# Exchanging the partition halves of the transposed q: copies on VectorE in the place of DMA transfers

## The chip, the core and the metric

The kernel runs on one core of a Trainium2 chip. The metric is the device time of one execution in microseconds. Before the change it is 370.4 us, the median of three runs (370.34 to 371.06).

A core has five engines, each with an in-order queue of its own: TensorE (PE, matmuls; PEld is its weight load), VectorE (DVE), ScalarE (ACT), GpSimd (POOL) and SyncE (SP). DMA transfers run beside them; here SP issues transposes, swaps and stores, and POOL issues the loads. SBUF and PSUM are memories of 128 partitions; matmul results go to PSUM and are moved on by VectorE or ScalarE.

## What is computed

An attention without softmax (squared ReLU), and then a feed-forward layer with exact GELU:

```
# q, k, v: 8 batches x 12 heads x 448 positions x 64, float32
scores = q @ k.T / sqrt(64)
attn   = maximum(scores, 0) ** 2 / 448
x      = attn @ v                      # then to (8 * 448) x 768
out    = gelu(x @ w_in) @ w_out        # w_in 768 x 2048, w_out 2048 x 768
```

## The kernel before

**Tiling.** The work goes by batch b (8), by group g of four heads (3 to a batch) and by step i (7 to a group). A step computes scores with 64x64 matmuls, of which four use the 128x128 array at once: pairs of heads lie in partitions 0 to 63 and 64 to 127 (`fn_qk`, L741, into the PSUM tile `ps`). ScalarE (L753) or VectorE (L755) makes the ReLU into `a_sq`, VectorE squares it (L762), and after seven steps 28 matmuls multiply by v (L802, into `pav`). Casts of `pav` (L517 on VectorE, L519 on ScalarE) give `xT`. The feed-forward layer follows in pieces that are woven between the attention steps: `psh` (L854) and its GELU (L864), then groups of 256 rows with sums on VectorE (`s_sb`, L1153), products (`pso`, L1172) and passes into `osb` (L1206), which SP stores (L1133). The later batches' first layer (`pb`, L998) and row groups use a scheme with seven products in the place of eight. `osb` has 3 buffers, `ps` and `pav` share 3 PSUM buffers, `psh` and `pso` share 2.

**The transposed q.** Scores need q and k with the head dimension on the partitions. For batches 0 and 1 TensorE transposes them (`tp`, L639 and L611). For batches 2 to 7 DMA does (`add_T_dma`): for each group SP issues a transpose of k into `kT` and one of q into a segment of `qT` (both L666). A segment is 128 partitions by 896 bf16 columns. The segment that the transpose fills (the even one, number 2g) has two of the heads' halves in partitions 0 to 63 and the others in 64 to 127. Both matmul halves need both, so a second segment (2g + 1) holds the same data with the partition halves exchanged. It is made by two transfers of 64x896 within `qT` (L686 and L687), here called the swap of a group: there are 6 x 3 = 18. `q_pair` reads both segments in one access, so a group's first scores wait for its swap (`Tq[b, g, c] = (even, both)`).

**The gates.** Before POOL loads q and k of a later batch over the natural tiles `nq` and `nk`, it makes a small copy (`add_gate`, L709) that waits for the transposes of the batch before. For batch 2 the copy reads the odd segment, which the swap writes; for the later batches it reads the even segment. In batches 3 to 6 POOL's first gate is the one for the last group, so a batch's burst of loads starts when that group's even transpose has landed. SP's next transposes wait for those loads.

**The order.** A small scheduler with planned times for each operation builds the program, but here the order is written out: `ORDER` is a list of words such as `D215` or `S230`, a letter for the engine (P, A, D, G, S for TensorE, ScalarE, VectorE, GpSimd, SP) and the operation's number. `place` follows it, and each engine's queue gets its operations in that sequence. The planned times of an operation (engine, time on the engine, time to the result) therefore change nothing in the built order. `mode="X"` marks SP's transposes and swaps for the planner's account of DMA.

The lines that are named later: L517 and L519 are the two branches of the helper `copy` on VectorE and ScalarE; L463 and L552 are the loads of q and k, L570 those of v, L486 those of w_out; L666 the transposes; L686 and L687 the swap; L709 the gates; L1133 the stores.

Of the kernel before, what the change touches and what calls it, by code (L numbers as in the profile page):

```python
# [69 lines left out]
T_STEP = 1.4  # L70
T_TIME = 3.6
T_LOAD = 1.0
SWAP_STEP = 0.9
SWAP_TIME = 3.0


def cols(half):
# [21 lines left out]
D212 A250 P257 D193 A214 A256 D194 P265 D218 S230 A258 D185 P201 D215 A266 G237 S231 G239 P225  # L99
A202 S233 A203 P276 P279 P267 D226 S235 A277 A227 P291 D280 P288 P294 S236 A268 P356 G240 A295  # L100
D289 G153 G238 P350 A357 G149 P348 G270 A292 A351 P285 P300 P303 G272 A349 P354 G241 A301 P364
A304 A355 P312 P318 P362 A365 P370 D319 D281 A363 D296 P358 A313 D290 A286 P282 P306 A371 P315
# [3 lines left out]
A340 A299 D393 A334 D394 P330 P324 P309 D329 P387 D419 A331 D335 A385 S400 S402 A310 D395 D311  # L106
S386 A325 P342 P336 S401 P321 D397 D388 A343 D332 P421 A322 D337 A323 S403 P423 D420 D338 D422
S405 P446 P443 D341 P449 P425 D424 D344 A450 S404 P427 G413 D444 G275 A426 G409 S406 S389 D447
P429 D326 D428 P452 P455 P345 A456 D453 P440 P437 D445 P431 D430 A441 D560 P433 D346 A347 D432
S435 P473 A438 P461 P470 D434 S436 P509 G407 G408 G410 A471 D474 P513 D448 G412 A462 S542 D457  # L110
A510 G411 P479 D454 P476 P464 G415 A514 P519 D472 D442 G414 A465 D439 P517 A520 D477 P515 A480
D451 A518 S541 P485 P467 P458 A468 P491 A516 S545 P511 D459 A486 D561 P523 A492 D487 S543 A512
D460 P503 P494 P500 D563 A524 P525 D463 S544 A495 D466 P521 D469 A526 D481 P531 S546 D504 A522
D478 P527 A532 D501 P537 D475 S548 A528 D505 P529 D502 A538 D493 S547 P488 P497 P482 S549 A498
D489 P606 G556 P600 G552 G416 P535 A483 A530 G550 P533 D601 G551 A607 D484 A536 G553 D490 G555
P539 D496 G554 D499 P609 G559 P603 P506 G558 A604 D610 G557 P624 A534 P639 D562 P564 A540 D605
A507 P566 A640 D625 D565 D508 P615 P612 P618 D567 P568 A616 D613 P570 D617 A569 D611 D614 P572
S705 D619 P657 D571 P627 P636 S704 P574 D580 D573 A637 D620 P576 D608 A658 D575 S578 A628 P584
D581 S708 D638 D577 P586 D583 S579 D582 P630 D602 P633 P621 S706 D626 A634 D631 P651 A585 S707
P642 P588 D632 D587 A643 S709 D659 P590 D629 A652 A622 D641 D591 P648 A623 D644 P666 P663 A589  # L120
S711 D653 P592 D635 A664 S710 G719 P594 G715 A649 D667 D593 S712 P654 P660 P645 A655 D661 P769
P763 D595 P596 S598 D725 A770 G713 G714 A646 P672 D764 G716 D597 S599 P674 G718 D665 D650 A673
G717 G721 A647 D656 P772 P778 P775 G720 D662 A675 P678 S868 A776 D779 P676 D668 A773 D771 P766
D777 P787 P669 S867 A767 D788 A679 P781 P790 A677 D774 P682 A670 D723 D768 P684 A782 A671 D724
A683 D765 P680 D783 A791 D780 P796 P799 P784 A681 S871 A800 D797 P793 P802 P688 S869 D803 D804
S870 D798 D789 S872 D792 S874 S873 S875 G882 G722 A785 A685 P686 A794 A689 A786 P811 P823 P805
A687 P690 D795 A806 P692 A691 D824 P698 D726 A812 D807 A693 P696 D801 A699 P814 P817 P808 A697
A815 D818 P820 P906 G878 P694 A809 G876 G877 P702 D907 G879 A695 A810 G881 P700 G880 A821 G884
A703 P826 P829 D822 P912 A701 P727 A827 P729 D828 A728 D813 P731 A913 D730 A830 D816 P733 D819
# [3 lines left out]
D923 D926 D754 P757 D932 D908 S980 P939 P948 P927 D758 S981 A940 D949 P960 P945 D941 P835 A928  # L133
S983 D756 D950 A946 P759 A929 S761 D961 S985 D947 P957 P954 P951 A836 D760 S984 A958 D955 P963
P966 P839 D956 A952 S762 D953 S986 A967 P837 D959 A840 P969 D964 P972 P987 A838 D888 P841 A973
P843 D988 D965 A842 D989 P845 A970 D962 A844 D974 P847 D971 A846 D1067 P1002 D968 P990 P975 A1003
# [262 lines left out]
def kernel(  # L399
# [9 lines left out]
    nc = tc.nc  # L409
# [93 lines left out]
    def q_seg(b, n):  # L503

        return get_T(b)[0][:, SEG * n : SEG * n + SEG]
# [9 lines left out]
    def copy(eng, dst, src):  # L515
        if eng == "DVE":
            V.tensor_copy(dst, src)  # L517
        else:
            A.copy(dst, src)  # L519

    def e_copy(n, psum=4):
# [4 lines left out]
    sch = Scheduler({"w": 3, "a": NA, "f": 2, "osb": 3, "s1": 1, "s2": 1, "s3": 1, "s4": 1,  # L526
                     "p": 1})
# [10 lines left out]
    QK, SQ, AV, X, GL = {}, {}, {}, {}, {}  # L538
# [61 lines left out]
    def old_T(b):  # L600
        return [o for (bb, *_), o in QK.items() if bb == b - 2]
# [56 lines left out]
    def add_T_dma(b, after):  # L658


        after = [list(x) for x in after]

        def turn(dst, src, deps):
            return sch.add(
                (("SP", T_STEP, T_TIME),),
                lambda e: nc.sync.dma_start_transpose(dst(), src()),  # L666
                deps + old_T(b) + after.pop(0), mode="X",
            )
# [12 lines left out]

        def swapped(g):
            def fn(e):
                src = q_seg(b, 2 * g)
                to = q_seg(b, 2 * g + 1)
                nc.sync.dma_start(to[:64], src[64:])  # L686
                nc.sync.dma_start(to[64:], src[:64])  # L687

            return fn

        for g in range(G):
            op = turn(k_dst(g), k_src(g), list(ld_k[b, g]))
            for i in range(NK):
                Tk[b, g, i] = (op, op)
            lands = list(dict.fromkeys(ld_q[b, g, c] for c in range(NC)))
            even = turn(q_dst(g), q_src(g), lands)
            both = sch.add(
                (("SP", SWAP_STEP, SWAP_TIME),), swapped(g), [even] + after.pop(0), mode="X"
            )
            for c in range(NC):  # L700
                Tq[b, g, c] = (even, both)

# [839 lines left out]
```

## Time and profile before

| what | value |
|---|---|
| median of 3 runs | 370.4 us |
| the profiled execution: time, span | 370.97 us, 368.8 us |
| ScalarE, GpSimd busy | 52%, 17% |
| granted TensorE clock | full in all slices |
| `qT<-qT` transfers (the swaps) | 36 of 112 KB, 2.5 us median to landing |
| all DMA traffic | 47.10 MB, 128 GB/s mean |
| POOL's waits at the gates for `qT<-nq`, `qT<-qT` | 86.7 us, 21.7 us |
| longest VectorE wait between 120 us and 160 us | 3.17 us, for a store of `osb` |

The page of a profile gives each engine's busy time, the same in 40 slices (a digit is tenths of the slice, 9 is 90% or more), the chain of work that ended last, and groups of instructions by line. A group's row ends with its busy time, the mean ns of one instruction, and the idle time before them with what ended it. In a timeline the columns are start, length (both us), engine, line, operation, what it writes and reads, shapes, count, and in brackets the idle time before it with what ended that. VectorE's lengths overlap: the next instruction can start a little before the recorded end of the one before. DMA-issuing instructions are marked with a q behind the engine's name (SPq); their length is that of the issue, not of the transfer.

### The profile page before, as it was taken

To read this page: it belongs to the slowest core of one execution; us is meant where nothing else is said; L and a number is where in the kernel's file an instruction comes from. 1 tells how busy PE (TensorE), PEld (TensorE's weight loads), DVE (VectorE), ACT (ScalarE), POOL (GpSimd) and SP (SyncE) were. 2 spreads that over 40 slices of the span, in tenths; PEclk is the share of its full clock that TensorE was granted. 3 is DMA by queue.
4 is the path that set the end of the run, shared out by engine and by line. 5 is a ranking of instruction groups with operands and counts; after the bars stand their busy time and mean duration, and the time that the engine had idled before them with its cause. 6 is when DMAs were issued, how large, how long until landed. Compare 5 with 4: busy or idle time off the path is not lost.

```text
span 368.8 us, 8478 instructions
## 1 busy us (share of the span) xinstructions
PE 358.4 (97%) x3560; PEld 222.6 (60%) x3560; DVE 287.8 (78%) x480; ACT 191.9 (52%) x312; POOL 62.3 (17%) x101
## 2 busy tenths in 40 slices
PE   8889999999999999899999999999999999999995
PEld 7665554455544555454555544467898777867663
DVE  3998862589996899698759999999977866667753
ACT  4987868637377544658666366860514124232200
POOL 8565116130240150050051000000000000000000
PEclk9999999999999999999999999999999999999999
DMA  9999999999999999999999970000300202022233
GB/s 166 198 199 201 191 159 145 208 196 187 198 192 195 173 158 171 232 153 192 156 151 222 199 161 2 2 2 0 88 2 0 88 20 67 2 85 87 85 85 88
DMA packets 75046, 47.10 MB, mean 128 GB/s; under 512 B 38528, under 2 KB 71552, under 8 KB 75008
## 3 DMA queue, kind: packets, MB, share of 16 engines
q0 software_dynamic: 32912, 22.47, 42.7%
q1 hardware_dynamic: 41456, 23.59, 32.3%
q8 instruction: 28, 0.46, 0.5%
q10 hardware_dynamic: 640, 0.51, 0.4%
q14 instruction: 10, 0.08, 0.1%
HBM read 45.61 MB, written 11.01 MB: 154 GB/s over the span
## 4 chain that ended last, share of the span: by engine, by line
PE 88%; DMA 5%; DVE 3%; POOL 1%; issue 1%; DVEq 0%; POOLq 0%; SPq 0%
PE pso L1172 29%; PE psh L854 26%; PE pb L998 13%; PE ps L741 9%; PE pav L802 9%; PE pso L1267 3%; DMA out_dram<-osb 3%; DMA v_sb<-in_v_dram 2%; DVE a_sq L762 1%; DVE a_sq L755 1%; DVE osb L1206 1%; POOL nk L552 1%; POOL nq L463 1%; PE tp L639 0%; DVE s_sb L1153 0%
## 5 line engine op out<-in xcount | busy, mean ns | idle before, releaser
L753 ACT ACTIVATE a_sq<-ps 128x896 bf16<-128x896 f32 (+1 forms) x116 | 102.5, 923 | 46.6 <-PE ps L741 43.5
L762 DVE TENSOR_TENSOR a_sq<-a_sq 128x896 bf16<-128x896 bf16 x169 | 97.0, 616 | 7.9 <-ACT a_sq L753 7.7
L854 PE MATMUL psh<-xT,win_sb 128*128 128x448 bf16 (+1 forms) x516 | 96.3, 340 | 0.0
L854 PEld LDWEIGHTS <-win_sb 128*128 128x128 bf16 x516 | 47.9, 98 | 46.1 <-issue 10.0
L755 DVE TENSOR_SCALAR a_sq<-ps 128x896 bf16<-128x896 f32 (+1 forms) x53 | 57.1, 1079 | 18.0 <-PE ps L741 17.8
L1172 PEld LDWEIGHTS <-s_sb 128*128 128x128 bf16 x424 | 40.7, 98 | 25.6 <-issue 1.7
L864 ACT ACTIVATE h_sb<-psh 128x448 bf16<-128x448 f32 x80 | 43.5, 550 | 22.1 <-PE psh L854 21.7
L741 PE MATMUL ps<-qT,kT 64*64 64x448 bf16 (+1 forms) x756 | 47.6, 336 | 1.3 <-issue 0.6
L1035 DVE TENSOR_TENSOR part<-pb,part 128x448 f32<-128x448 f32 x60 | 35.2, 619 | 13.5 <-PE pb L998 11.4
L1172 PEld LDWEIGHTS <-h_sb 128*128 128x128 bf16 x312 | 29.7, 98 | 22.2 <-issue 4.6
L802 PE MATMUL pav<-a_sq,v_sb 64*64 64x448 bf16 (+1 forms) x756 | 36.3, 329 | 2.1 <-issue 1.2
L1172 PE MATMUL pso<-wout_sb,h_sb 128*128 128x384 bf16 x208 | 38.1, 326 | 0.0
L1172 PE MATMUL pso<-wout_sb,s_sb 128*128 128x384 bf16 (+2 forms) x216 | 38.1, 320 | 0.0
L1172 PE MATMUL pso<-t_sb,s_sb 128*128 128x384 bf16 x208 | 38.1, 326 | 0.0
L1206 DVE TENSOR_TENSOR osb<-pso,p_sb 128x384 f32<-128x384 f32 x39 | 21.6, 553 | 15.6 <-PE pso L1172 10.6
L741 PEld LDWEIGHTS <-kT 64*64 64x64 bf16 x756 | 18.5, 105 | 21.1 <-issue 16.2
L802 PEld LDWEIGHTS <-v_sb 64*64 64x64 bf16 x756 | 21.2, 107 | 13.8 <-issue 3.0
L998 PEld LDWEIGHTS <-win_sb 128*128 128x128 bf16 x288 | 27.5, 98 | 2.9 <-issue 0.7
L1044 ACT ACTIVATE h_sb<-part 128x448 bf16<-128x448 f32 x36 | 18.4, 576 | 19.0 <-DVE part L1035 18.9
L519 ACT CAST xT<-pav 128x448 bf16<-128x448 f32 (+1 forms) x38 | 18.3, 500 | 7.8 <-PE pav L802 6.4
L709 POOL COPY gate<-qT 128x16 bf16<-128x16 bf16 x15 | 3.7, 247 | 108.4 <-DMA qT<-nq 86.7
L998 PEld LDWEIGHTS <-ws 128*128 128x128 bf16 x216 | 20.8, 98 | 1.2
(57 smaller groups left out, 298.1 us busy)
## 6 DMA issues: line engine op xcount, KB each, us to landing
nk<-in_k_dram POOLq DMA_DIRECT2D x23, 224.0 KB, 9.2
nq<-in_q_dram POOLq DMA_DIRECT2D x21, 224.0 KB, 9.9
qT<-qT SPq DMA_DIRECT2D x36, 112.0 KB, 2.5
v_sb<-in_v_dram POOLq DMA_DIRECT2D x5, 672.0 KB, 9.8
out_dram<-osb SPq DMA_DIRECT2D x8, 336.0 KB, 3.1
v_sb<-in_v_dram POOLq DMA_DIRECT2D x9, 224.0 KB, 9.7
out_dram<-osb SPq DMA_DIRECT2D x7, 288.0 KB, 3.1
out_dram<-osb SPq DMA_DIRECT2D x8, 240.0 KB, 2.9
```

The costliest lines, as they stand in the source:

```text
L741: nc.tensor.matmul(ps[64 * j : 64 * j + 64, e, x * w : x * w + w], kT[r, g, i * 128 + 64 * j : i * 128 + 64 * j + 64], moving, start=True, ...
L753: A.activation(ar, ps, AF.Relu, scale=c_att)
L755: V.tensor_scalar(ar, ps, c_att, 0.0, op0=mybir.AluOpType.mult, op1=mybir.AluOpType.max,)
L762: V.tensor_mul(box["a2"][:, :, :used], ar, ar)
L802: nc.tensor.matmul(pav[0][o2 : o2 + 64, e, :w], vt[b][r, 2 * g + e, bass.ts(i, D)], box["a2"][r, y, o : o + w], start=(i == 0), stop=(i == ...
L854: nc.tensor.matmul(ph[:, x * n : x * n + n], win_sb[:, kd, bass.ts(m + x, 128)], xT[b][:, kd, c], start=(kd == 0), stop=(kd == KD - 1),)
L864: A.activation(h_ring()[:, m : m + nm, o + c.start : o + c.stop], box[0][:, :S].rearrange("p (x n) -> p x n", x=nm), AF.Gelu,)
L998: nc.tensor.matmul(bank[name][:, y, z * HS : z * HS + HS], w[:, k, bass.ts(mm, 128)], right()[:, k], start=first and k == 0 and z == 0, st ...
L1035: V.tensor_add(get(to), ps(name), get(other))
L1044: A.activation(h_ring()[:, m : m + 2, o + half[c].start : o + half[c].stop], src().rearrange("p (x n) -> p x n", x=2), AF.Gelu,)
L1172: nc.tensor.matmul(box[bank][:, n0:n1], left()[:, kf], right()[:, kf, n0:n1], start=bool(need) and kf == 0, stop=kf == K2 - 1, skip_group_ ...
L1206: V.tensor_add(out()[:, n0:n1], box[bank][:, n0:n1], other()[:, n0:n1])
```

## The change

The two transfers of a swap become two copies of the same shape (64x896 bf16, SBUF to SBUF, from partitions 64 to 127 into 0 to 63 and the other way), made by the helper `copy`. The operation may go to VectorE or ScalarE; in `ORDER` each of the 18 words leaves SP's sequence and comes in again, as a D word, 3 to 60 words later. All other words keep their sequence. The planner's figures for the swap change with it.

```
-SWAP_STEP = 0.9
-SWAP_TIME = 3.0
+SWAP = (("DVE", 0.6, 0.72), ("ACT", 1.8, 1.95))
...
-... P265 D218 S230 A258 D185 P201 D215 ...
+... P265 D218 A258 D185 P201 D230 D215 ...
...
             def fn(e):
                 src = q_seg(b, 2 * g)
                 to = q_seg(b, 2 * g + 1)
-                nc.sync.dma_start(to[:64], src[64:])
-                nc.sync.dma_start(to[64:], src[:64])
+                copy(e, to[:64], src[64:])
+                copy(e, to[64:], src[:64])
...
-            both = sch.add(
-                (("SP", SWAP_STEP, SWAP_TIME),), swapped(g), [even] + after.pop(0), mode="X"
-            )
+            both = sch.add(SWAP, swapped(g), [even] + after.pop(0))
```

The 18 words are 230, 233, 236 (batch 2), 400, 403, 406 (batch 3), 543, 546, 549, 706, 709, 712, 869, 872, 875 and 980, 983, 986 (batches 4 to 7). In the built program each pair of copies waits for the semaphore of its even transpose; in batches 4 to 7 the first pair of a batch also waits for a gate on the same buffer two batches earlier. The gates of batch 2 wait for VectorE in the place of a transfer.

More of the change, by code (lines that the diff above doesn't have):

```diff
@@ L98 @@
 S228 D209 A262 D197 P213 P222 P192 D200 S232 A248 P263 D221 A223 D206 P249 D224 A264 D188 P255
[L99 to L102, printed above, removed]
+D212 A250 P257 D193 A214 A256 D194 P265 D218 A258 D185 P201 D230 D215 A266 G237 S231 G239 P225
+A202 A203 P276 P279 P267 D233 D226 S235 A277 A227 P291 D280 P288 P294 A268 P356 G240 A295 D289
+G153 G238 P350 A357 G149 P348 G270 A292 A351 P285 P300 P303 G272 A349 P354 G241 A301 P364 A304
+A355 P312 P318 P362 A365 P370 D319 D281 A363 D296 P358 A313 D236 D290 A286 P282 P306 A371 P315
 P352 A359 D307 P360 A353 P376 A361 P368 A316 A377 D317 P372 D314 A369 D308 P366 D293 A373 P378
@@ L105 @@
 D302 D287 G269 S398 P327 P339 D320 P297 G271 D396 G155 A328 D383 P333 G274 P384 D381 G273 D298
[L106 to L109, printed above, removed]
+A340 A299 D393 A334 D394 P330 P324 P309 D329 P387 D419 A331 D335 A385 S402 A310 D395 D311 S386
@@ L110 @@
+A325 P342 P336 S401 P321 D397 D400 D388 A343 D332 P421 A322 D337 A323 P423 D420 D338 D422 S405
+P446 P443 D341 P449 P425 D424 D344 A450 S404 P427 G413 D444 G275 A426 G409 S389 D403 D447 P429
+D326 D428 P452 P455 P345 A456 D453 P440 P437 D445 P431 D430 A441 D406 D560 P433 D346 A347 D432
 S435 P473 A438 P461 P470 D434 S436 P509 G407 G408 G410 A471 D474 P513 D448 G412 A462 S542 D457
 A510 G411 P479 D454 P476 P464 G415 A514 P519 D472 D442 G414 A465 D439 P517 A520 D477 P515 A480
-D451 A518 S541 P485 P467 P458 A468 P491 A516 S545 P511 D459 A486 D561 P523 A492 D487 S543 A512
@@ L113 @@
[L113 to L116, printed above, removed]
+D451 A518 S541 P485 P467 P458 A468 P491 A516 S545 P511 D459 A486 D561 P523 A492 D487 A512 D460
+P503 P494 P500 D563 A524 P525 D463 S544 A495 D466 P521 D469 A526 D481 P531 D504 A522 D478 P527
@@ L117 @@
+A532 D501 P537 D475 S548 A528 D505 P529 D543 D502 A538 D493 S547 P488 P497 P482 A498 D489 P606
+G556 P600 G552 G416 P535 A483 A530 G550 P533 D546 D601 G551 A607 D484 A536 G553 D490 G555 P539
+D496 G554 D499 P609 G559 P603 P506 G558 A604 D610 G557 P624 A534 P639 D549 D562 P564 A540 D605
 A507 P566 A640 D625 D565 D508 P615 P612 P618 D567 P568 A616 D613 P570 D617 A569 D611 D614 P572
 S705 D619 P657 D571 P627 P636 S704 P574 D580 D573 A637 D620 P576 D608 A658 D575 S578 A628 P584
-D581 S708 D638 D577 P586 D583 S579 D582 P630 D602 P633 P621 S706 D626 A634 D631 P651 A585 S707
@@ L120 @@
[L120 to L123, printed above, removed]
-D777 P787 P669 S867 A767 D788 A679 P781 P790 A677 D774 P682 A670 D723 D768 P684 A782 A671 D724
-A683 D765 P680 D783 A791 D780 P796 P799 P784 A681 S871 A800 D797 P793 P802 P688 S869 D803 D804
@@ L126 @@
[L126 to L129, printed above, removed]
+D581 S708 D638 D577 P586 D583 S579 D582 P630 D602 P633 P621 D626 A634 D631 P651 A585 S707 P642
+P588 D706 D632 D587 A643 D659 P590 D629 A652 A622 D641 D591 P648 A623 D644 P666 P663 A589 S711
@@ new lines @@
+D653 P592 D635 A664 S710 G719 P594 G715 A649 D667 D593 P654 P660 P645 A655 D661 P769 P763 D709
+D595 P596 S598 D725 A770 G713 G714 A646 P672 D764 G716 D597 S599 P674 G718 D665 D650 A673 G717
+G721 A647 D656 P772 P778 P775 G720 D662 A675 P678 S868 A776 D779 P676 D712 D668 A773 D771 P766
+D777 P787 P669 S867 A767 D788 A679 P781 P790 A677 D774 P682 A670 D723 D768 P684 A782 A671 D724
+A683 D765 P680 D783 A791 D780 P796 P799 P784 A681 S871 A800 D797 P793 P802 P688 D803 D804 S870
+D798 D789 D792 S874 S873 G882 G722 A785 A685 P686 A794 A689 A786 P811 P823 P805 A687 P690 D795
@@ L130 @@
+A806 P692 A691 D824 P698 D726 A812 D807 A693 P696 D869 D801 A699 P814 P817 P808 A697 A815 D872
+D818 P820 P906 G878 P694 A809 G876 G877 P702 D907 G879 A695 A810 G881 P700 G880 A821 G884 A703
+P826 P829 D822 P912 A701 P727 A827 P729 D828 A728 D875 D813 P731 A913 D730 A830 D816 P733 D819
 D825 P921 D831 P909 P832 A910 D922 P918 P936 D732 G885 P735 D734 A833 G883 D911 A919 D834 P924
@@ L132 @@
 D740 S742 P749 D917 A748 D935 S979 P751 D914 A943 D920 D750 S978 P753 D944 A752 D746 S982 P755
[L133 to L136, printed above, removed]
+D923 D926 D754 P757 D932 D908 P939 P948 P927 D758 S981 A940 D949 P960 P945 D941 P835 A928 D980
+D756 D950 A946 P759 A929 S761 D961 S985 D983 D947 P957 P954 P951 A836 D760 S984 A958 D955 P963
+P966 P839 D956 A952 S762 D953 A967 P837 D959 A840 P969 D964 P972 P987 A838 D888 P841 A973 P843
+D988 D965 A842 D989 P845 A970 D986 D962 A844 D974 P847 D971 A846 D1067 P1002 D968 P990 P975 A1003
 D991 A848 P993 P996 P851 D976 A994 A977 P999 D997 P1014 P1005 A852 D1004 P849 D995 D992 P853 D886
```

## The prediction

> **What bounds the kernel now.** I read the busy times and the slices first, then the chain that ended last, then the engines' timelines around the eighteen places where the change acts.
>
> ```profile
> span 368.8 us, 8478 instructions
> PE 358.4 (97%) x3560; PEld 222.6 (60%) x3560; DVE 287.8 (78%) x480; ACT 191.9 (52%) x312; POOL 62.3 (17%) x101
> ...
> PE   8889999999999999899999999999999999999995
> ...
> DVE  3998862589996899698759999999977866667753
> ...
> DMA  9999999999999999999999970000300202022233
> ...
> PE 88%; DMA 5%; DVE 3%; POOL 1%; issue 1%; DVEq 0%; POOLq 0%; SPq 0%
> ```
>
> TensorE is the bound: 97% busy, nine tenths or more in every slice but the start, one in the middle and the last. The chain has 3% of VectorE and 5% of DMA. So time can be won only where TensorE stands, and time is lost wherever something that it needs comes later. From 50 us to 240 us, where the change acts, the trace has TensorE standing twice, close together:
>
> ```profile
> 148.22 1.69 DVE L762 TENSOR_TENSOR a_sq<-a_sq 128x896 bf16<-128x896 bf16 x3
> 153.08 0.56 DVE L1206 TENSOR_TENSOR osb<-pso,p_sb 128x384 f32<-128x384 f32 x1 [3.17 <-DMA out_dram<-osb]
> ...
> 153.69 1.46 PE L1172 MATMUL pso<-t_sb,h_sb 128*128 128x384 bf16 x8 [1.11 <-DVE osb L1206]
> ...
> 156.29 1.52 PE L802 MATMUL pav<-a_sq,v_sb 64*64 64x448 bf16 x28 [0.64 <-DVE a_sq L755]
> ```
>
> A store of `osb`, issued at 142.4, landed at 152.96, behind loads that POOL had issued between 128.4 and 134.6 and of which the last landed at 153.06. VectorE waited 3.17 us for the buffer, TensorE 1.11 + 0.64 = 1.75 us. That is all that can be won here.
>
> **What the change removes.** The 36 transfers of L686 and L687 (112 KB each, 4.03 of the 47.1 MB) and SP's work for them: 18 x (0.48 + 0.59) = 19.2 us of issuing by their medians, and 17.7 us in which SP stood at L686 for the transpose that the swap reads, holding up the transposes and stores queued behind it:
>
> ```profile
> SPq L686 <- DMA qT<-nq: 17.7, 11, 8.2
> ...
> 116.33 4.06 SPq L666 DMA_TRANSPOSE qT<-nq  x1
> 120.89 0.50 SPq L686 DMA_DIRECT2D qT<-qT  x1
> 121.44 0.58 SPq L687 DMA_DIRECT2D qT<-qT  x1
> 122.12 1.28 SPq L666 DMA_TRANSPOSE kT<-nk  x1
> 123.50 0.55 SPq L686 DMA_DIRECT2D qT<-qT  x1
> 124.09 0.59 SPq L687 DMA_DIRECT2D qT<-qT  x1
> 124.73 1.33 SPq L666 DMA_TRANSPOSE qT<-nq  x1
> ```
>
> Here, without the four swap issues, the transpose of 124.73 can go at about 121.8 (120.39 + 1.3 for the k transpose and its gap), 2.9 us sooner. It landed at 127.76 and POOL's gate followed at 127.88; so the burst of loads starts about 2.9 us sooner, ends near 150, and the `osb` store that lands with it does too. VectorE, free for that buffer at 149.9 and by then about 1.6 us later for the reasons below, would find it free, and TensorE's 1.75 us go. I take -1.75; bounds 0 (the store is late all the same) and -1.75. The gates of batch 2 (L709), which waited for the swap itself (POOL: 21.7 us for `qT<-qT`), open at about 52.0, 53.2 and 66.9 by the VectorE times below, where they opened at 52.8, 57.5 and 69.2. Nothing on TensorE waits for what they release, so that counts as nothing; were it late instead, the next to wait would be the batch-3 transposes on SP.
>
> **What it adds.** 36 copies, 64x896 bf16 in SBUF, in pairs, on VectorE's in-order queue. The built order has all 18 pairs on VectorE and none on ScalarE, and the other instructions of VectorE in their old order. The wait is for the even transpose (and a gate's read, long over). By the trace of before, the transpose had landed 0.8 to 3.8 us before VectorE came free at each of the 18 places (1.6 or more at 17 of them, and 0.8 at 51.95, where 2.8 us of idle time follow), and the SP relief makes it earlier. So I count no wait. Were a pair to wait, it would hold the ReLUs, squares and evacuations behind it, and TensorE through them.
>
> The trace of before has no such copy. The nearest rows:
>
> ```profile
> L762 DVE TENSOR_TENSOR a_sq<-a_sq 128x896 bf16<-128x896 bf16 x167 | 96.5, 618 | 7.9 <-ACT a_sq L753 7.7
> ...
> L517 DVE COPY kT<-tp 128x896 bf16<-128x896 bf16 x5 | 3.1, 618 | 0.0
> ...
> L517 DVE COPY qT<-tp 128x448 bf16<-128x448 bf16 x6 | 2.2, 386 | 1.1 <-PE tp L639 1.1
> ```
>
> Back to back, the 618 ns instructions start every 0.535 us (three take 1.69). The slope, (618 - 386)/448 = 0.52 ns per element, leaves 0.07 us fixed in that step. So one copy costs between 0.07 (the fixed part alone) and 0.535 (the PSUM copy's rate), a pair 0.14 to 1.07. Between them I take the figure in the kernel's own planner, 0.60 for the pair, because its other figures meet the rows: 0.07 + 896/2/960 = 0.537 for the copies from PSUM against 0.535, and 0.07 + 2x448/960 = 1.00 for the ReLU of L755 against a step of 1.00 (119.08 to 120.08). 18 x 0.60 = 10.8 us on VectorE.
>
> The Trainium skill, "VectorE: DVE Perf Modes" (the perf-mode tier table and the errata's cycle row), lets an SBUF-to-SBUF bf16 copy run four elements a cycle: (58 + 896/4)/0.96 GHz, an estimate of 0.29 us each. By it the sum would be the same within 0.2 us; no row of before shows that rate.
>
> **How much of it reaches TensorE.** I carry VectorE's lateness along its timeline: +0.60 at each pair, minus each idle gap, and where an output goes to TensorE (or through ScalarE) I compare it with the margin, which is the consumer's start minus the producer's end minus 0.06 (the shortest hand-over seen is 153.64 to 153.69). What exceeds the margin delays TensorE, and VectorE is then late by the margin alone. Seven pairs vanish in idle gaps: three before 68.2 (2.83 and 1.32 idle), two near 124.6 and 126.5 (0.78, 0.80), two before 181.1 (1.65). So does one before 189.8 (0.90). The others:
> - 91.35, 97.49, 102.44: 1.2 late, less 0.86 idle at 100.43 leaves 0.33; +0.60 is 0.93 at the `xT` cast of 103.03, which through two ScalarE steps has 0.18 to the scores at 105.3: 0.75 lost (and 0.01 before).
> - 131.34 and 147.21: 0.10 at 134.09, then 0.16 around 144 (margins of 0.14 and 0.06): 0.26.
> - 157.62, 163.43: 0.32 at 159.68 (margin 0.28), 0.34 at 165.49: 0.66.
> - 209.80, 211.80, 219.85: these sit where VectorE has no gap,
>
> ```profile
> 209.80 0.55 DVE L1206 TENSOR_TENSOR osb<-pso,osb 128x384 f32<-128x384 f32 x1
> 210.26 0.61 DVE L762 TENSOR_TENSOR a_sq<-a_sq 128x896 bf16<-128x896 bf16 x1
> 210.80 1.08 DVE L755 TENSOR_SCALAR a_sq<-ps 128x896 bf16<-128x896 f32 x1
> ```
>
> 1.18 late against margins of 0.88 (the square of 211.80) and 0.14 (the ReLU of 213.00, needed at 214.29): 0.02 + 0.30 + 0.67, and 0.26 at 221.87. Together 1.25.
>
> Sum 0.76 + 0.26 + 0.66 + 1.25 = 2.9 us. The same account with pairs of 0.14, 0.30, 0.45, 0.70 and 1.07 us gives 0.1, 0.6, 1.6, 3.9 and 7.9.
>
> One more cost. The only VectorE instruction of before that goes from SBUF to SBUF with one input ran while POOL issued a load: the `nk` cast at 4.87 took 0.92 us for 512 columns where the f32 rows of one element a cycle (448 in 0.62, 896 in 1.09) give 0.69, and POOL's issue beside it 0.98 instead of 0.72 to 0.75. Four or five pairs fall into POOL's bursts, at their old or their earlier place (97.5, 102.4, 125.7, 131.3, 157.6). At 0.23 us each that is 1.0 us on VectorE, of which, by the step from pairs of 0.60 to 0.70 (18 x 0.1 = 1.8 us more, 0.97 lost), some 54% arrives: +0.55; bounds 0 and 1.75 (a whole issue of 0.72 each).
>
> The Trainium skill, "SBUF — State Buffer" (Who interferes with whom), makes this a rule: a VectorE copy in a two-port mode and a GpSimd instruction exclude each other for a whole instruction. That speaks against the change. The cast's row agrees in direction but shows 0.23, not a whole issue.
>
> **The sum.** 2.9 + 0.55 - 1.75 = +1.7 us. The profiled execution took 370.97 us (368.8 of span, 2.2 around it), so 372.7 by it; it lies 0.57 above the median of 370.4, and against the median I say 372.1.
>
> **Rivals.**
> - Faster: the freed SP queue outweighs the copies. Place: the SP queue from 116 to 128 and the stand at 153. It decides once a pair costs under about 0.47 us, where the account gives 1.75. With pairs of 0.30: 0.6 - 1.75 = -1.2, 369.2. For it: the whole 1.75 us hangs on loads that really follow the swaps. Against: 0.30 a pair is half the planner's figure. Chance 0.18.
> - The stand at 153 stays, because the store waits for VectorE too: 2.9 + 0.55, 373.8. For it: VectorE runs without a gap from 134.9 to 149.9 and writes the store's last input in that stretch. Chance 0.17.
> - The copies are dear: pairs of 1.07 (the rate of every bf16 row in the trace), or each colliding pair waiting out a whole POOL issue. 7.9 - 1.75 is +6.2, 376.6; the second, 2.9 + 1.75 - 1.75 = +2.9, 373.3. Chance 0.18, a third of it the first.
> - A pair waits for its transpose: one that lands 5 us later than now would hold VectorE some 3 us, 375. Against: the margins above. Chance 0.04.
> - That the change does not do what it says is excluded by the built order.
>
> **How the numbers follow.** The forecast has chance 0.43; its own range, pairs of 0.5 to 0.7, is 371.2 to 373.1. A measurement of this kernel cannot tell 0.2%, 0.74 us, from no change. Faster by more: nearly all of the first rival, 0.16. Within 0.2% (369.7 to 371.1): the edge between it and the forecast, 0.12. Slower: 0.72. The range leaves out a tenth on each side: the better half of the fast rival below 369.4, and pairs near 1.07 above 376.0.
>
> **What would show it.** Copies `qT<-qT` on L516 of VectorE near 0.3 us to the next start, some longer beside POOL's loads; SP without L686 waits; loads of batch 5 from about 125.5; no idle on VectorE at an `osb` for a store; TensorE gaps or late scores near 103, 160, 166 and 214, ended by VectorE. Wrong if the copies take 0.5 us or more each, if the store still lands near 153, or if VectorE stands before a copy for a `qT<-nq` transfer.

## The result and the profile after

The changed kernel takes 374.92 us, the median of four runs (373.8 to 375.07), against 370.37 us for the kernel before in four runs beside them (369.8 to 371.06). The ratio is 1.0116, with a 95% interval of 0.9% to 1.4% slower: [1.0089, 1.0142]. The profiled execution took 374.96 us with a span of 373.2 us, against 370.97 and 368.8. The direction was forecast. The size was not: +4.5 us in the place of +1.7.

The page of the kernel after: the busy times, the slices of three rows, and the shares of the chain that ended last.

```profile
span 373.2 us, 8468 instructions
PE 361.2 (97%) x3560; PEld 223.4 (60%) x3560; DVE 302.7 (81%) x516; ACT 192.1 (51%) x312; POOL 63.5 (17%) x101
...
PE   8889999999999999999999999999999999999995
...
DVE  3988882689996999998879999999977766667753
...
DMA  9999979998998994899918750000300202022233
...
PE 55%; DVE 7%; issue 0%; DVEq 0%
```

VectorE has 36 instructions and 14.9 us more. The chain is followed back to 138 us only, so its shares add up to 62%; in that part DMA has none of it, where the store of `osb` alone had 3% of the span before, and VectorE has 7%, where it had 3% in the whole chain before. TensorE still shows nines everywhere, also in the slice in the middle that was an eight. So the stand is gone, and what was lost is lost in portions too small for a digit.

The stand at 153 us, in VectorE's and in TensorE's timeline of the kernel after (the same square of three, the same `osb` sum and the same two groups of matmuls as shown before, L759, L1203, L1169 and L799 now):

```profile
151.76 1.69 DVE L759 TENSOR_TENSOR a_sq<-a_sq 128x896 bf16<-128x896 bf16 x3
153.40 0.56 DVE L1203 TENSOR_TENSOR osb<-pso,p_sb 128x384 f32<-128x384 f32 x1
```

```profile
155.29 1.46 PE L1169 MATMUL pso<-t_sb,h_sb 128*128 128x384 bf16 x8
...
157.09 1.11 PE L799 MATMUL pav<-a_sq,v_sb 64*64 64x448 bf16 x20
```

No bracket stands behind any of the four rows: neither engine waited. SP's queue shows why. Its row of waits for the swaps is gone, and its transposes follow each other:

```profile
109.06 1.31 SPq L665 DMA_TRANSPOSE qT<-nq  x1
110.46 1.38 SPq L665 DMA_TRANSPOSE kT<-nk  x1
111.94 1.66 SPq L665 DMA_TRANSPOSE qT<-nq  x1
113.69 1.25 SPq L665 DMA_TRANSPOSE kT<-nk  x1
115.03 1.25 SPq L665 DMA_TRANSPOSE qT<-nq  x1
```

The last of them stood at 124.73 before. It is 9.7 us earlier, not 2.9, because the relief of batches 2 and 3 adds up in the one queue: the gates of batch 3 had already opened at 95.17 in the place of 99.25. The first gate of the burst is at 119.11 instead of 127.88, the burst's last load lands at 142.5 instead of 153.06, and the two stores of `osb` land at 148.7 and 149.4 instead of 151.7 and 153.0.

What is lost is in the new rows: the group of copies, and one stretch of VectorE's timeline in batch 7, where it has no gap.

```profile
L516 DVE COPY qT<-qT 64x896 bf16<-64x896 bf16 x36 | 14.7, 409 | 0.7
```

```profile
211.35 0.61 DVE L759 TENSOR_TENSOR a_sq<-a_sq 128x896 bf16<-128x896 bf16 x1
211.97 0.79 DVE L516 COPY qT<-qT 64x896 bf16<-64x896 bf16 x2
212.80 0.56 DVE L1203 TENSOR_TENSOR osb<-pso,osb 128x384 f32<-128x384 f32 x1
213.27 0.61 DVE L759 TENSOR_TENSOR a_sq<-a_sq 128x896 bf16<-128x896 bf16 x1
213.80 1.08 DVE L752 TENSOR_SCALAR a_sq<-ps 128x896 bf16<-128x896 f32 x1
214.92 0.79 DVE L516 COPY qT<-qT 64x896 bf16<-64x896 bf16 x2
215.74 0.62 DVE L759 TENSOR_TENSOR a_sq<-a_sq 128x896 bf16<-128x896 bf16 x1
```

The first square starts at 211.35 and the sum behind the copies at 212.80, 1.45 us later. Without the copies the next instruction would have started 0.53 us after the square. The pair cost 0.92 us here, and that is also the median over the pairs of the trace.

The same matmul in both traces tells where TensorE came late. In this table (us, read from the starts of the matmuls in order) a step is a change of the lateness; the account is the prediction's own, done again with pairs of 0.92 us.

| place (time before) | forecast, pairs of 0.60 | account, pairs of 0.92 | measured |
|---|---|---|---|
| start-up, 26.0, ahead of all swaps | | | +0.54 |
| batch 3: 100.4, 105.1, 105.3 | 0.76 | 1.65 | 0.62 + 0.37 + 0.63 |
| batch 4: 126.1, 135.2, 149.0 | 0.26 | 0.71 | 0.18 + 0.35 + 0.19 |
| the stand: 153.7, 156.3 | -1.75 | | -1.28 - 0.81 |
| batch 5: 160.6, 166.8, 182.4 | 0.66 | 1.35 | 0.66 + 0.46 + 0.15 |
| batch 7: 211.0, 213.4, 214.3, 222.9 | 1.25 | 2.21 | 0.36 + 0.65 + 0.53 + 0.59 |

The measured steps of the copies are 5.7 us, the regained stand is 2.1 us, and with the scatter of the start TensorE is 4.2 us late at 223 us, of 4.4 us by which the span grew.

### The profile page after: what moved, and what is told of

It is laid out like the page before. It is cut to its first block, busy times and chain, and to the rows that moved or that the text cites. A ratio compares the mean times of both kernels' runs of the same rounds, so it can differ in the third digit from the quotient of the medians.

```text
span 373.2 us, 8468 instructions
## 1 busy us (share of the span) xinstructions
PE 361.2 (97%) x3560; PEld 223.4 (60%) x3560; DVE 302.7 (81%) x516; ACT 192.1 (51%) x312; POOL 63.5 (17%) x101
## 2 busy tenths in 40 slices
DMA packets 72166, 42.97 MB, mean 115 GB/s; under 512 B 37952, under 2 KB 68672, under 8 KB 72128
## 4 chain that ended last, share of the span: by engine, by line
PE 55%; DVE 7%; issue 0%; DVEq 0%
PE pso L1169 28%; PE pb L995 13%; PE psh L851 7%; PE ps L738 4%; PE pav L799 3%; DVE a_sq L759 2%; DVE a_sq L752 2%; DVE qT L516 1%; DVE osb L1203 1%; DVE s_sb L1150 0%; DVE xT L516 0%; DVE xs L962 0%; DVEq L1534 0%
## 5 line engine op out<-in xcount | busy, mean ns | idle before, releaser
L759 DVE TENSOR_TENSOR a_sq<-a_sq 128x896 bf16<-128x896 bf16 x169 | 97.6, 616 | 8.1 <-ACT a_sq L750 7.7
L1169 PEld LDWEIGHTS <-s_sb 128*128 128x128 bf16 x424 | 40.7, 98 | 26.2 <-issue 2.4
L738 PE MATMUL ps<-qT,kT 64*64 64x448 bf16 (+1 forms) x756 | 49.3, 336 | 2.7 <-ACT a_sq L750 0.9
L1169 PEld LDWEIGHTS <-h_sb 128*128 128x128 bf16 x312 | 29.8, 98 | 20.6 <-issue 3.0
L799 PE MATMUL pav<-a_sq,v_sb 64*64 64x448 bf16 (+1 forms) x756 | 37.2, 329 | 2.2 <-issue 1.2
L1169 PE MATMUL pso<-wout_sb,s_sb 128*128 128x384 bf16 (+2 forms) x216 | 38.1, 320 | 0.2 <-DVE osb L1203 0.2
L1169 PE MATMUL pso<-wout_sb,h_sb 128*128 128x384 bf16 x208 | 38.1, 326 | 0.0
L1169 PE MATMUL pso<-t_sb,s_sb 128*128 128x384 bf16 x208 | 38.1, 326 | 0.0
L1203 DVE TENSOR_TENSOR osb<-pso,p_sb 128x384 f32<-128x384 f32 x39 | 21.6, 553 | 11.2 <-PE pso L1169 10.2
L799 PEld LDWEIGHTS <-v_sb 64*64 64x64 bf16 x756 | 21.5, 107 | 14.5 <-issue 4.3
L706 POOL COPY gate<-qT 128x16 bf16<-128x16 bf16 x15 | 5.2, 346 | 104.1 <-DMA qT<-nq 82.5
```

The lines of the kernel that those rows point to most:

```text
L738: nc.tensor.matmul(ps[64 * j : 64 * j + 64, e, x * w : x * w + w], kT[r, g, i * 128 + 64 * j : i * 128 + 64 * j + 64], moving, start=True, ...
L759: V.tensor_mul(box["a2"][:, :, :used], ar, ar)
L799: nc.tensor.matmul(pav[0][o2 : o2 + 64, e, :w], vt[b][r, 2 * g + e, bass.ts(i, D)], box["a2"][r, y, o : o + w], start=(i == 0), stop=(i == ...
L1169: nc.tensor.matmul(box[bank][:, n0:n1], left()[:, kf], right()[:, kf, n0:n1], start=bool(need) and kf == 0, stop=kf == K2 - 1, skip_group_ ...
L1203: V.tensor_add(out()[:, n0:n1], box[bank][:, n0:n1], other()[:, n0:n1])
```

## The experiments

The first theory: VectorE's time for the copies makes the whole loss, and the freed SP queue gives back the stand at 153 us. Each run stands beside runs of the kernel before on the same chip (median 370.63 us for the first four experiments, 371.04 for the others that were timed); the ratios are against those.

**Only two swaps become copies.** From the kernel before, the swaps 543 and 546 (batch 4, groups 0 and 1) go to VectorE at the places that the change gives them:

```
-... D487 S543 A512 D460 ... P531 S546 D504 ...
+... D487 A512 D460 ... P531 D504 ... P529 D543 D502 ... P533 D546 D601 ...
```

> Only the swaps of groups 0 and 1 of batch 4 are copies on VectorE; the other 16 stay DMA transfers on SP. My theory: the gain of the change (2.09 us of TensorE's lateness given back at the stand near 153 us) comes from the SP queue ahead of batch 4's last even transpose, which these two swaps held up, and these two pairs fall into idle gaps of VectorE (TensorE lost 0.18 us there in the changed kernel). So 370.4 - 1.9 = 368.5 us, and VectorE has no wait for a store of osb. Rival: the gain needs the DMA engines relieved of all swaps, or the SP queue freed in all batches; then the stand stays and the time is 370.2 to 370.8.

Measured: 369.52 us (368.47 to 370.75, 12 runs), ratio 0.9968 [0.9943, 0.9993]. It is faster, by less than expected. Its trace has the stand gone, by the narrowest margin seen: the gate is only 1.0 us sooner (126.86), the stores land at 151.76 and 151.97, and VectorE starts the sum at 152.09. The wait ahead of it is put down to TensorE's scores and no longer to a store, but the store had landed only 0.12 us before.

```profile
149.78 1.15 DVE L767 TENSOR_TENSOR a_sq<-a_sq 128x896 bf16<-128x896 bf16 x2
152.09 0.56 DVE L1211 TENSOR_TENSOR osb<-pso,p_sb 128x384 f32<-128x384 f32 x1 [1.16 <-PE ps L746]
```

TensorE regains 1.29 + 0.75 us there. In this one execution it had lost 1.0 us between 75.5 and 87 us, ahead of the two copies. The trace says for what: VectorE's first sum of w_out, shown here from the kernel before and then from this run, waits for a load.

```profile
76.07 0.95 DVE L1108 TENSOR_TENSOR t_sb<-wout_sb 128x1536 bf16<-128x1536 bf16 x1
```

```profile
77.50 0.96 DVE L1113 TENSOR_TENSOR t_sb<-wout_sb 128x1536 bf16<-128x1536 bf16 x1 [1.34 <-DMA wout_sb<-in_moe_w_out_dram]
```

The load landed at 75.73 in the profiled execution of the kernel before, 0.34 us ahead of the sum, and at 77.47 here. POOL issues it behind a gate of batch 2. The same wait, with 1.0 to 1.7 us of TensorE's time, stands in the traces of the three other runs below that keep all swaps on SP. In the changed kernel that gate opens at 54.93 in the place of 57.50 and the load lands at 70.55; there, and in the four other traces in which batches 2 and 3 have no transfers, it lands more than 5 us before the sum and TensorE loses nothing at this place. So the transfers have a second place at which they can cost time, and the profiled execution of the kernel before just missed it.

**The swaps of batch 4 back on SP.** From the changed kernel, 543, 546 and 549 are transfers again, at their old places in SP's sequence.

```
-... P529 D543 D502 ... P533 D546 D601 ... P639 D549 D562 ...
+... D487 S543 A512 ... P531 S546 D504 ... S547 P488 P497 P482 S549 A498 ...
```

> The changed kernel with the three swaps of batch 4 back as DMA transfers on SP; the other 15 are copies on VectorE. My theory: the stand at the osb store returns (+2.1 us) and batch 4's copies no longer delay TensorE (0.18 + 0.35 + some 0.1 less): 374.9 + 1.5 = 376.4 us. Rival: the relief comes from the other batches or from the DMA traffic in general: 374.9 - 0.6 = 374.3 us, with no stand.

Measured: 373.53 us (373.19 to 375.28, 9 runs), ratio 1.0079 [1.005, 1.0109]. The expectation failed: the stand did not come back. The first gate of the burst is at 121.55, still 6.3 us sooner than before, from the relief of batches 2 and 3 alone, and VectorE goes through the place without a wait:

```profile
151.00 1.69 DVE L767 TENSOR_TENSOR a_sq<-a_sq 128x896 bf16<-128x896 bf16 x3
152.63 0.56 DVE L1211 TENSOR_TENSOR osb<-pso,p_sb 128x384 f32<-128x384 f32 x1
```

With the run above this says that the gain at this place is a threshold, not an amount. Taking either two swaps of batch 4 or those of the batches ahead off SP is enough, and the rest of the relief buys nothing here.

**The copies beside the transfers.** From the kernel before, all swaps stay on SP, and 36 copies of 64x640 (smaller, so that a spare tile fits) go to VectorE at the 18 places of the change; nobody reads them.

```
+                V.tensor_copy(spare[:64], src[64:, :640])
+                V.tensor_copy(spare[64:], src[:64, :640])
```

> The kernel before with its swaps as DMA transfers on SP, and at the 18 places of the change pairs of VectorE copies of 64x640 bf16 from the even segment into a spare tile that nothing reads. My theory: VectorE's time alone makes the loss. A pair of 64x896 took 0.92 us in the changed kernel; 256 columns fewer at the slope of four elements a cycle make it 0.79, and the account of lateness against margins gives 4.8 us for that; the stand at 153 us stays. So 370.4 + 4.8 = 375.2 us. Rival: the loss comes from the moved order of DMA and loads, not from VectorE's time: 370.4 to 371.0 us.

Measured: 374.75 us (372.94 to 376.2, 4 runs), ratio 1.0101 [1.0046, 1.0156]. The copies make the kernel slower with nothing else touched, by about as much as the change does. The four runs lie apart, two near 373.1 and two near 376.2, and the trace is of one of the slower two: 1.2 us of its lateness come from the wait for w_out told above, ahead of 87 us. What the copies add is read from the steps behind that, some 4.5 us together. They take 322 and 356 ns, TensorE gets late at the same matmuls (at 210.98, 213.35, 214.29 and 222.89 by 0.27, 0.53, 0.50 and 0.45 us), and the stand is there, since SP has its swaps:

```profile
151.45 1.68 DVE L772 TENSOR_TENSOR a_sq<-a_sq 128x896 bf16<-128x896 bf16 x3
155.94 0.56 DVE L1216 TENSOR_TENSOR osb<-pso,p_sb 128x384 f32<-128x384 f32 x1 [2.81 <-DMA out_dram<-osb]
```

**No exchange at all.** From the kernel before, the transfers go and nothing takes their place; the order is that of before. This leaves out a part of the computation: the scores read both heads' halves from the even segment alone, and so do the gates of batch 2.

```
-        x = q_seg(b, 2 * g + e)[64 * e : 64 * e + 64, o : o + HS]
-        step = -SEG if e else SEG
+        x = q_seg(b, 2 * g)[64 * e : 64 * e + 64, o : o + HS]
+        step = HS if o < SEG - HS else -HS
...
-                nc.sync.dma_start(to[:64], src[64:])
-                nc.sync.dma_start(to[64:], src[:64])
+                pass
```

> The kernel before without the 36 transfers and without copies; the scores read the even segment alone, so both halves of a head pair are multiplied with data of one segment. The shape and number of the matmuls stay. My theory: only the stand at the osb store can be won, 370.4 - 2.1 = 368.3 us, so the 36 copies cost the changed kernel 6.6 us. Rival: the swaps on DMA cost TensorE nothing, the stand stays: 370.4 us, and the copies cost 4.5 us.

Measured: 368.26 us (367.49 to 369.37, 10 runs), ratio 0.9927 [0.99, 0.9953]. This is the price of both sides. The transfers on SP cost the kernel before some 2.4 us (370.63 to 368.26; the stand is 2.1 of it), and the copies cost the changed kernel 374.92 - 368.26 = 6.7 us. In the two traces TensorE ends 6.8 us apart. 1.05 us of that lie ahead of the first swap, where nothing was changed; the other 5.8 agree with the 5.7 read from the steps.

**The price of a copy by itself.** The kernel before, followed by rows of squares and copies on VectorE with nothing else running. It tells whether crossing the partitions, or the size, makes the copies dear.

```
+    def cross(n):
+        for _ in range(n):
+            V.tensor_copy(x2[:64], x0[64:])
+            V.tensor_copy(x2[64:], x0[:64])
...
+    square(3)
+    cross(3)
+    square(3)
+    for _ in range(3):
+        V.tensor_copy(x2[:64], x0[:64])
+        V.tensor_copy(x2[64:], x0[64:])
+    square(3)
+    for _ in range(4):
+        V.tensor_copy(x2, x0)
...
+    nc.gpsimd.tensor_copy(x2[:64], x0[64:])
+    nc.gpsimd.tensor_copy(x2[64:], x0[:64])
```

> The kernel before, and after its last operation rows of copies and squares on VectorE alone, in spare SBUF, so only the steps between their starts are read here. My theory: a 64x896 bf16 copy costs a step of 0.40 us because a copy does not start before the instruction ahead of it has ended, where squares start every 0.535 us with a length of 0.62; a pair between squares then costs 0.92 us, the same with source and destination in the same partitions. Rival: the exchange of partition halves makes the copies slow; then copies in the same partitions step by 0.30 us. With POOL issuing two loads beside six pairs, single copies grow by 0.1 to 0.3 us.

Measured, in VectorE's timeline behind the kernel's end (L1525 and L1526 cross the partitions, L1534 and L1535 do not, L1538 moves all 128):

```profile
369.33 0.39 DVE L1525 COPY mic<-mic 64x896 bf16<-64x896 bf16 x1
369.73 0.39 DVE L1526 COPY mic<-mic 64x896 bf16<-64x896 bf16 x1
370.15 1.94 DVE L1521 TENSOR_TENSOR mic<-mic 128x896 bf16<-128x896 bf16 x3
372.10 0.39 DVE L1525 COPY mic<-mic 64x896 bf16<-64x896 bf16 x1
...
374.58 1.95 DVE L1521 TENSOR_TENSOR mic<-mic 128x896 bf16<-128x896 bf16 x3
376.45 0.38 DVE L1534 COPY mic<-mic 64x896 bf16<-64x896 bf16 x1
376.86 0.39 DVE L1535 COPY mic<-mic 64x896 bf16<-64x896 bf16 x1
...
378.52 0.39 DVE L1535 COPY mic<-mic 64x896 bf16<-64x896 bf16 x1
378.92 1.94 DVE L1521 TENSOR_TENSOR mic<-mic 128x896 bf16<-128x896 bf16 x3
380.78 1.67 DVE L1538 COPY mic<-mic 128x896 bf16<-128x896 bf16 x4
382.37 1.94 DVE L1521 TENSOR_TENSOR mic<-mic 128x896 bf16<-128x896 bf16 x3
...
389.35 3.16 DVE L1521 TENSOR_TENSOR mic<-mic 128x896 bf16<-128x896 bf16 x3
```

A copy takes 0.39 us in all three forms, and the next starts 0.40 to 0.43 us after it, whether it crosses the partitions or not, on 64 partitions or on 128. A pair from 369.33 to 370.15 is 0.82 us. These rows follow each other less closely than those of the kernel, since most of them wait for a signal of the one before, as they write the same places again: even squares start every 0.66 us here, and every 0.535 in the kernel. So the equal steps do not say that crossing costs nothing.

The places where a square and a copy meet, and where neither waits for a signal, do tell. The crossing copy of 372.10 starts 0.01 us after the square ahead of it has ended. The copies of 376.45 and 380.78, which keep their partitions, start 0.08 us before that end, and the square of 382.37 starts 0.08 us before the end of the whole copy. Behind the copy of partitions 64 to 127 (378.52) the square does wait for the end. Crossing does not make a copy longer, then, but it ends the overlap with its neighbours; the expectation that it would make no difference failed in this. Inside the kernel it is the same: a square that is followed by its like hands on after 0.535 us, but one that is followed by a crossing copy runs to its end, 0.62 us and a gap of 0.01 to 0.03. That is 0.10 us more, and 0.82 + 0.10 is the 0.92 us of the changed kernel.

The loads that this run was to hold beside copies ran at 324 us, long before them, so it told nothing of collisions; the last run was made for that. The last row, three squares beside two copies on GpSimd, comes up again there.

**The swaps as transfers that POOL issues.** All 18 leave SP without a copy on VectorE: the words change from S to G at their old places.

```
-... P265 D218 S230 A258 D185 P201 ...
+... P265 D218 G230 A258 D185 P201 ...
...
-                nc.sync.dma_start(to[:64], src[64:])
-                nc.sync.dma_start(to[64:], src[:64])
+                if e in ("SP", "POOL"):
+                    q = nc.sync if e == "SP" else nc.gpsimd
+                    q.dma_start(to[:64], src[64:])
+                    q.dma_start(to[64:], src[:64])
...
```

> The 18 swaps as DMA transfers issued by POOL in the place of SP, each where SP had it in the planned order; no copies on VectorE. My theory: what can be won is the stand at the osb store, and it goes once batch 5's loads start 1 us sooner than in the kernel before, or more; POOL's own 1.4 us for a pair of issues delay them by less than the freed SP queue brings: 368.3 to 369.0 us. Rival: a swap that POOL issues queues behind loads in the DMA engines (9 to 12 us to land), and scores wait for it in batch 3 or 4: 371 us or more.

Measured: 373.86 us (371.82 to 376.01, 7 runs), ratio 1.008 [1.0046, 1.0113]. My expectation failed and the rival held, though in batch 2 and not in batch 3 or 4. POOL's timeline at batch 2, and TensorE's wait there:

```profile
55.10 1.55 POOL L485 DMA_DIRECT2D wout_sb<-in_moe_w_out_dram  x2 [0.28 <-issue]
56.63 0.57 POOL L687 DMA_DIRECT2D qT<-qT  x1
```

```profile
60.47 0.38 PE L746 MATMUL ps<-qT,kT 64*64 64x448 bf16 x4
63.51 0.93 PE L746 MATMUL ps<-qT,kT 64*64 64x448 bf16 x8 [2.65 <-issue]
```

Four transfers are issued right behind the loads of w_out and take 6.3 to 6.8 us to land (the median over all 36 is 3.9), where the median of SP's was 2.5. The loads ahead of them seem to matter more than the engine that issues: the two that POOL issued ahead of the loads took 2.7 and 3.9 us, and in the kernel before SP's own took 5.2 and 5.3 us behind the loads of w_out (issued at 63.2 and 63.7) and 6.4 to 6.6 at 148.7. The scores wait for them: 2.85 us of lateness here, 0.34 at 95.3. Another 1.4 us go between 75.5 and 87, where VectorE waits for loads. And POOL, in order, stands up to 10.4 us for the transpose that a swap reads, with the next batch's loads behind it. The burst's first gate is at 130.65, not sooner than before, and VectorE still waits 2.09 us for a store at 156.94.

**The copies moved to gaps.** From the changed kernel, all 18 pairs stay on VectorE, and 12 of them go to places where the timeline of before shows VectorE idle, or where what follows has a margin: 403 and 406 behind the cast that feeds the scores of 105.3, 549 to 130.3, 706 into the place of the former stand, and the others to 160.2, 172.9, 181.1, 185.9, 187.7, 207.7, 222.9 and 232.5. Two of the twelve:

```
-... S389 D403 D447 P429 ... A441 D406 D560 P433 D346 A347 D432 ...
+... S389 D447 P429 ... A441 D560 P433 D346 A347 D403 D432 ... A471 D406 D474 ...
```

> The changed kernel with 12 of its 18 pairs at other places of VectorE's order, chosen by the account of idle gaps and margins with 0.92 us for a pair: behind the xT cast of batch 3's last group, in the gaps of batches 6 and 7, at the place of the stand. My theory: the loss is the price of a pair less the cover at its place. The account gives 1.4 us lost in the place of 6.1, and without the stand 368.3 + 1.4 = 369.7 us. Rival: the copies cost their sum in VectorE's time wherever they stand: 374 to 375 us.

Measured: 369.27 us (368.83 to 370.49, 12 runs), ratio 0.9961 [0.9941, 0.9982]. The same 36 copies that cost 6.7 us in one order cost about 1.0 us in another (369.27 against the 368.26 of the run without an exchange; 1.3 by the two ratios). It is faster than the kernel before. What is left of their lateness in the trace is 0.20 us at 131.8, 0.15 at 166.8, 0.16 at 209.6 and 0.29 at 224.2.

**Copies where there are gaps, transfers where there are none.** As the run above, but 709, 980, 983 and 986 are transfers on SP again. SP issues 709 at 147.8, behind the stores that the stand waited for, and the others from 204 on, so its work for them holds up no burst that matters.

```
-... D923 D926 ... P927 D980 D758 ... D983 D991 ... A858 D986 D1059 ...
+... D923 D926 ... D908 S980 P939 ... S983 D756 ... D953 S986 A967 ...
```

> As the spread places, but the four pairs that no gap covers (batch 5 group 1, batch 7) are DMA transfers on SP again. My theory: 0.4 us lost to copies, no stand: 368.3 + 0.4 = 368.7 us. Rival: with four swaps on SP the stand returns in part or the remaining pairs collide with POOL's loads: 369.5 to 371 us.

Measured: 368.54 us (368.23 to 369.01, 10 runs), ratio 0.9933 [0.9912, 0.9954]. It beats both kernels and is 0.3 us from the run that does not exchange at all: the trace has 28 copies, 0.17 us of lateness from them at 131.8, and the stand regained in full (-1.25 and -0.81).

**Copies beside POOL's loads.** Again rows behind the kernel before: copies, then squares, beside loads that POOL issues, and then copies beside two 64x896 copies on GpSimd.

```
+    square(3)
+    nc.gpsimd.tensor_copy(m2[:, :16], x1[:, :16])
+    for c in range(6):
+        load(m2, c, c)
+    cross(8)
...
+    for c in range(3):
+        load(m, 3 + c, c)
+    for _ in range(6):
+        V.tensor_mul(x2, x0, x0)
...
+    nc.gpsimd.tensor_copy(m3[:64, :SEG], x1[64:])
+    nc.gpsimd.tensor_copy(m3[64:, :SEG], x1[:64])
+    cross(4)
```

> The kernel before, followed by rows on VectorE beside GpSimd's work: after three squares, eight pairs of 64x896 copies beside six loads that POOL issues (0.7 us each); six squares beside three more loads; four pairs beside two 64x896 copies made by GpSimd itself. Away from POOL's work a copy took 0.39 us and stepped every 0.41, a square 0.62. Theory (a copy and an issuing load hold each other up for part of the time only): copies beside the loads take 0.45 to 0.67 us, mean some 0.1 to 0.15 more than alone, and POOL's issues hardly grow. Rival (they exclude each other for a whole instruction): copies beside loads take 0.39 + up to 0.72 us, or none overlaps an issue, and the eight pairs take 6 x 0.7 = 4 us more than their 6.6. Second rival (a load costs a copy nothing; the longer copies of the changed kernel had another cause): all stay at 0.39. Beside GpSimd's own copies the squares at the end of the earlier row took 1.24 us instead of 0.62; the pairs are expected to take 0.8 us a copy by the same, or 0.39 if only instructions with two inputs are held up.

Measured, first in VectorE's timeline and then in POOL's:

```profile
370.19 0.43 DVE L1526 COPY mic<-mic 64x896 bf16<-64x896 bf16 x1
370.65 0.69 DVE L1525 COPY mic<-mic 64x896 bf16<-64x896 bf16 x1
371.37 0.66 DVE L1526 COPY mic<-mic 64x896 bf16<-64x896 bf16 x1
372.07 0.66 DVE L1525 COPY mic<-mic 64x896 bf16<-64x896 bf16 x1
372.76 0.39 DVE L1526 COPY mic<-mic 64x896 bf16<-64x896 bf16 x1
...
376.05 3.92 DVE L1548 TENSOR_TENSOR mic<-mic 128x896 bf16<-128x896 bf16 x6
...
381.62 1.01 DVE L1526 COPY mic<-mic 64x896 bf16<-64x896 bf16 x1
```

```profile
367.91 4.60 POOL L1533 DMA_DIRECT2D mic<-in_q_dram  x6 [0.30 <-POOL mic L1539]
...
376.67 2.08 POOL L1533 DMA_DIRECT2D mic<-in_q_dram  x3
```

The theory held. Of the nine copies that start while POOL issues loads, six take 0.43 to 0.69 us in the place of 0.39, and POOL's issues stretch a little too: six took 4.60 us, where the other three took 0.69 each. The eight pairs took 7.68 us (367.17 to 374.85) in the place of 16 x 0.42 = 6.7, some 0.16 us for each load. The rival with a whole issue of 0.7 us for each is excluded. The squares, with two inputs, did not notice the loads: six in 3.92 us is the step of 0.66 that they had alone in these rows.

## Why the forecast was right in direction and short in size

**The pair's price, the step that failed.** The prediction put a pair at 0.60 us, "the figure in the kernel's own planner", between 0.14 and 1.07. It measured 0.92. The planner's other figures met the rows of before because those rows were of instructions that overlap with the next of their kind; the copy starts after the end of what is ahead of it and does not hand on early, which the rows of single copies put down to its crossing the partitions. The carried account itself was sound: fed with 0.92 it gives 5.9 us, and batch by batch it lies within 0.1 us of the measured steps, 5.7 us in all. So the term of 2.9 us should have read 5.9. Undisturbed, the copies took 386 to 390 ns. (The transfers that went were 4.13 MB, from 47.10 to 42.97, not 4.03; nothing hangs on it.)

The Trainium skill, "VectorE: DVE Perf Modes" (the section on the errata), was cited for 0.29 us a copy. The sentence under its cycle table says that this row is too low and that about 150 cycles were measured in the place of the 58; (150 + 224)/0.96 GHz is an estimate of 0.39 us, and the trace agrees, with 0.39. The prediction took the table's row alone. Two copies of 0.39 us make 0.78, so the rest of the 0.92 is the gaps and the lost overlap.

**The stand.** Forecast -1.75 us, measured -2.09; that the stores would land in time was right. The forecast chain of causes was right in kind, and too small: 9.7 us sooner at the transpose and 8.8 at the gate, not 2.9, since only batch 4's relief was counted. The runs with two swaps and with batch 4 undone show that this error could not cost anything, as a relief of 1.0 us was already enough. That the stand is all that can be won holds for the profiled execution alone: it missed the wait for w_out by 0.34 us, and others did not.

**Collisions with POOL's loads.** Forecast 0.23 us each for four or five pairs, +0.55 on TensorE. In the changed kernel a few pairs show it, the dearest this one (VectorE's timeline, then POOL's):

```profile
125.00 1.19 DVE L516 COPY qT<-qT 64x896 bf16<-64x896 bf16 x2
```

```profile
124.53 0.74 POOL L462 DMA_DIRECT2D nq<-in_q_dram  x1
125.24 0.73 POOL L551 DMA_DIRECT2D nk<-in_k_dram  x1
```

1.19 us in the place of 0.79. Pairs at 53.5, 158.4 and 180.9 lost 0.1 us each, so VectorE lost some 0.8 us in all four. Of this no more than the step of 0.18 us at 126.1 is seen at TensorE apart from the copies' own account; the term was too large by a few tenths. The price of one collision was about right, and the rule that copy and issue lock each other out for a whole instruction (the Trainium skill, "SBUF — State Buffer", Who interferes with whom) is borne out in kind by the last run, with up to 0.30 us more for a copy, not 0.7. The same section says that a VectorE instruction with two inputs in SBUF contends with GpSimd instructions that read SBUF; the squares beside GpSimd's copies, 1.24 us in the place of 0.62, and beside loads unchanged, agree.

**What was counted as nothing.** No pair waited for its transpose, as forecast. The gates of batch 2 opened at 52.84, 54.93 and 67.81 (forecast 52.0, 53.2, 66.9); the lateness of VectorE is in the difference. To count this as nothing was right against the profiled execution, and in part luck: the load of w_out behind the second of these gates held up TensorE in four traces with the swaps of batch 2 on SP, and the earlier gates of the changed kernel put it out of reach.

**The rivals.** With -2.09 and +5.7 the kernel landed between the forecast and the rival of dear copies, nearer to that one. By its time alone the rival in which the stand stays (373.8) was nearest, but the trace shows no stand. The faster kernel that the first rival had in mind exists, but by the place of the copies and not by their price: the runs with moved copies have the same price and are faster than before.

**What stays open.** Half a microsecond of TensorE's lateness at 26 us lies ahead of everything that the change touches, and other executions show steps of up to 0.5 us of either sign between 25 and 31 us. I take it for scatter between executions; no run isolates it. How often the kernel before meets the wait for w_out is not known either, as only some of its executions were profiled. And why a change of partitions ends the overlap is not shown, only that it does.

## What to carry to other kernels

An engine that is 78% busy is not free: what a small instruction on it costs is decided by the gap or the margin at the place where it is put, and the same 36 copies cost 6.7 us in one order and 1.0 us in another. Price an instruction that the trace lacks by its full length plus the overlap that its neighbour loses, not by the step of instructions that overlap with their own kind. Relief of a queue counts until the next wait is met and not beyond; work that leaves one queue should go to each engine only as far as that engine has gaps.

## What the runs showed that I had not expected

- A 64x896 bf16 copy from SBUF to SBUF takes 0.39 us, and so does a 128x896 one: neither the number of partitions nor crossing them made it longer.
- A copy that crosses the partitions does not overlap with the instruction ahead, and ends the overlap of that one (it starts 0.01 us after the end of a square, where a copy that keeps its partitions starts 0.08 us before it): a pair costs 0.92 us between squares that hand on after 0.535, and 0.82 alone.
- Beside loads that POOL issues, copies grow by up to 0.30 us and squares by nothing; beside GpSimd's own copies (1.0 to 1.2 us each), both grow, to 1.0 and 1.24 us.
- The same transfer lands in 2.5 us (median) when SP issues it, and in 6.3 to 6.8 when POOL issues it behind loads; behind loads SP's own took 5.2 to 6.6.
- The transfers could cost time at two places: the stand at 153 us, and a load of w_out that lands 0.34 us before its use in one execution and 1.3 to 2.0 us too late in four others.
